# A weight row's tail and a unit's output in one transfer each, and W of a later unit begun at the head of a pass

## The chip, the cores and the metric

The kernel runs on one NeuronCore of a Trainium2 chip. That core has a matrix engine (TensorE, PE in the profile; PEld is its weight load), a vector engine (VectorE, DVE), a scalar engine (ScalarE, ACT), a general engine (GpSimd, POOL) and a sequencer that issues transfers (SyncE, SP). Transfers move between HBM and the on-chip memory SBUF through 16 DMA engines. Products of PE land in PSUM, a small memory in banks, from which DVE or ACT must read them before a bank can be used again.

The metric is the time of one execution on the device in microseconds (us), the median of several runs. Less is better.

## What is computed

Two parts follow each other. The first is a linear recurrence over 768 time steps for 4 batches and 8 heads of width 40; the second is a mixture of four experts, applied to the result as 3072 rows of 320.

```python
# attention: r, k, v, w, a, b are [batch 4, heads 8, seq 768, 40]
for t in range(S):
    y[:, :, t] = einsum('bhd,bhde->bhe', r_t, state)
    Sa = einsum('bhde,bhe->bhd', state, a_t)
    state = state * w_t[..., None] - einsum('bhd,bhe->bhde', Sa, b_t)
    state = state + einsum('bhd,bhe->bhde', v_t, k_t)
x = y.transpose(0, 2, 1, 3).reshape(3072, 320)

# mixture: w1 [4, 320, 1024], w2 [4, 1024, 320], p = domain_probs normalised by row
for e in range(4):
    h = maximum(x @ w1[e], 0)
    out += p[:, e:e+1] * (h @ w2[e])
```

All data are float32.

## The kernel before

**Units and passes.** The sequence is cut into 12 chunks of 64 tokens (L = 64). A unit is one chunk of two batches, so 128 rows on the 128 partitions; there are 24 units, two per chunk. The main loop (L1074 on) makes one pass per unit. Pass u works on several units at a time: it finishes the recurrence's step for one unit, prepares the next (`merge`, `begin_step`), advances the work inside the chunk of unit u + 2 (`within`, L402, with the substitution on POOL), and begins the loads of unit u + 3. Between these, at the places called `gap`, it issues pieces of the mixture for units that are already done, so that PE has products at all times.

**Loads of a unit.** Each input of a unit is loaded in one or two layouts. `load` (L198) brings W, B, K, V by tokens into `natW`, `natB`, `natK`, `natV` with two transfers each (L202). `load_raw` (L206) brings W, A, V, R by heads into `rawW`, `rawA`, `rawV`, `rawR`, four transfers each for W and A and eight each for V and R (L223); there is one buffer of each. DVE turns these round with a transpose (L241) into `G` (from rawW), `AT`, `VT` and `RT`. In the kernel before, pass u begins rawW, rawA, natW, natB, natK, natV of unit u + 3 in its middle, after `gap(1)`, and puts the transfers of rawV and rawR in a list called `later`, from which `mix` takes a few after each piece of the mixture.

**Step.** `step` (L628) makes `Y` of a unit (L707 adds, L712 scales with G). From the third chunk on, Y goes to the mixture's input `xT` with twelve transfers on SP from SBUF to SBUF (L736). On DVE, the same stage holds the work inside a later chunk: the reciprocal `gp` (L432), `n_tok` (L468), `k_tok` (L472), whose transposes PE makes (`pNT`, `pKT`, L79).

**Weights.** The first layer's weights don't stay on the chip. They stream as pieces: `load_piece` (L281) brings half an expert, 512 columns of w1 of 320 rows, into `w1p`, of which there are two buffers (the first pieces also use tiles called `sums`). Rows 0 to 255 come in one transfer of 512 KB, `main`, in runs of 2048 bytes. The last 64 rows, the tail, are held as two halves of the columns on partitions 0 to 63 and 64 to 127, and come in two transfers of 64 KB each, in runs of 1024 bytes (L300). 104 pieces are loaded: eight for each chunk, and sixteen for the first, whose two units are taken one after the other. In `up_last` the products on the tail come first for a piece: `ph` with lhsT = `last`, 64 x 64. The second layer's weights stay on the chip.

**Outputs.** `down_1` and `down_2` make the second layer's products, and DVE adds them into a tile `osb` of 128 rows for each unit (L786). `store` (L788) writes it to `out` in two transfers of 64 rows, 80 KB each, as the two batches lie apart in HBM. For the last chunk, `down_2_at_end` stores the last unit in two halves of the columns, the second with ACT as a second issuing engine.

**Order.** In the first passes (u < 5), and for what is put in `keep_in_program_order` (the pieces, the `later` transfers), each engine's order is as written. Elsewhere a scheduler places the instructions by its own estimate; so a change of a transfer's place in the code is not always a change of place on its engine. SP issues nearly all transfers, 1327 of 1336, one after the other; a transfer that waits, on a store's `osb` for instance, holds up those behind it. An even steady pass has natW, natV, twelve of xT, then pieces with natB, natK, rawW, rawV, rawA and rawR between; an odd pass has rawR, the four stores of a chunk, the last rawR, natW, natV, twelve of xT.

## Time and profile before

| | |
|---|---|
| median of three runs | 1124.0 us (1122.39 to 1124.98) |
| the profiled execution | 1122.36 us |
| its span, first to last instruction | 1120.2 us |
| granted TensorE clock, mean | 0.986 |
| transfers of w1p: mains and tails | 95 of 512 KB, 190 of 64 KB |
| transfers of pieces into `sums` tiles, mains | 9 of 512 KB |
| bytes read from HBM, written | 111.79 MB, 3.93 MB |

The profile is of one execution. Busy times are sums over the span; the DMA share is the mean over the core's 16 DMA engines. In a timeline a line gives the start, the duration, the engine, the line of the code, the operation, what it writes and reads, and how many instructions of the kind stand together; brackets at the end give the idle time before, and what ended it. For SP (SPq) the duration is that of issuing, not of moving the data.

## The change

There are three edits.

- The tail of a piece comes in one transfer. Its target is the 128 partitions of the tile's last 256 columns; its source is the 64 rows of w1 seen as two halves of columns, [2, 64, 256].
- `store` writes a unit's output in one transfer, from the 128 partitions of `osb` to an [2, 64, columns] view of `out`. Its parameter is now the issuing engine; at the end of the kernel the right half of the last unit is issued by ACT as a whole.
- rawW and natW of unit u + 3 are begun at the head of pass u, ahead of `run(w_next)` and so of the step whose end places xT. The rest, rawA, natB, natK and natV, is begun where all of them were. `begin(u + 3)` moves with it.

```diff
--- before.py
+++ after.py
@@ -290,13 +290,10 @@
         q.main = t[:, 0:2 * HF * P].rearrange("p (g c) -> p g c", g=2)
         q.last = t[:, 2 * HF * P:PIECE].rearrange("p (f c) -> p f c", c=P)
         cols = slice(x * HF * P, (x + 1) * HF * P)
-        moves = [(q.main, moe_w1[e, 0:2 * P, cols].rearrange("(g p) c -> p g c", p=P))]
-        for i in range(2):
-            half_cols = slice((2 * x + i) * HF // 2 * P, (2 * x + i + 1) * HF // 2 * P)
-            moves.append(
-                (q.last[i * DT:(i + 1) * DT], moe_w1[e, 2 * P:DM, half_cols].rearrange("d (f c) -> d f c", c=P))
-            )
-        for to, src in moves:
+        for to, src in (
+            (q.main, moe_w1[e, 0:2 * P, cols].rearrange("(g p) c -> p g c", p=P)),
+            (t[:, 2 * HF * P:PIECE], moe_w1[e, 2 * P:DM, cols].rearrange("d (i c) -> i d c", i=2)),
+        ):
             tc.keep_in_program_order(nc.sync.dma_start(out=to, in_=src))
         pieces.append(q)
 
@@ -785,10 +782,9 @@
         else:
             nc.vector.scalar_tensor_tensor(out=to, in0=p, scalar=sc, in1=to, op0=ALU.mult, op1=ALU.add)
 
-    def store(q, osb, cols=slice(0, DM), second=nc.sync):
-        for i, eng in enumerate((nc.sync, second)):
-            row = q.b[i] * S + q.c * L
-            eng.dma_start(out=out[row:row + L, cols], in_=osb[i * L:(i + 1) * L, cols])
+    def store(q, osb, cols=slice(0, DM), eng=nc.sync):
+        rows = out.rearrange("(b s) d -> b s d", b=B)[q.b[0]:q.b[1] + 1, q.c * L:(q.c + 1) * L, cols]
+        eng.dma_start(out=rows, in_=osb[:, cols])
 
     def outputs():
         return sb.tile([P, DM], FP32, name="osb", tag="osb", bufs=2)
@@ -1089,6 +1085,9 @@
         early = u < EARLY
         if early:
             begin_later(len(later))
+        if u + 3 < NU:
+            go(load_raw(begin(u + 3), "W"))
+            load(units[u + 3], "W")
         run(w_next, 99 if early else 1)
         run(s, 1)
         gap(0)
@@ -1116,8 +1115,8 @@
             gap(1)
 
         if u + 3 < NU:
-            go(load_raw(begin(u + 3), "WA"))
-            load(units[u + 3], "WBKV")
+            go(load_raw(units[u + 3], "A"))
+            load(units[u + 3], "BKV")
             later.extend(load_raw(units[u + 3], "VR"))
         run(w, 2)
```

`down_2_at_end` is the caller that passes the issuing engine; its text is unchanged: `store(qs[1], osb[1], right, nc.scalar)`.

## What the change was predicted to do

> **What bounds the kernel now.** I read the page's engine shares first, then busy time by stage, then the timelines of SP, VectorE (DVE) and TensorE (PE) over one pass, because the change touches only SP's transfers and the question is which wait on one of them reaches PE.

> ```profile
> span 1120.2 us, 38531 instructions
> PE 1076.8 (96%) x16100; PEld 961.0 (86%) x16100; DVE 757.0 (68%) x1553; ACT 353.2 (32%) x956; POOL 501.9 (45%) x1272
> q1 hardware_dynamic: 265416, 119.12, 44.0%
> ```
> ```profile
> 43.00:86.00 43.00, 38.61 (x632) 31.82 (x631) 24.73 (x64) 14.56 (x45) 2.50 (x6) 1.00 0.88 253
> 258.00:301.00 43.00, 39.99 (x532) 36.24 (x531) 28.88 (x57) 11.84 (x31) 19.81 (x51) 0.96 0.48 114
> 516.00:559.00 43.00, 43.00 (x670) 39.02 (x669) 31.37 (x64) 14.35 (x39) 21.80 (x56) 1.00 0.46 112
> 559.00:602.00 43.00, 42.85 (x671) 38.80 (x670) 31.22 (x64) 14.47 (x39) 22.00 (x56) 1.00 0.47 108
> ```

> The second fence is busy time by stage: stretch, length, then PE, weight loads, DVE, ACT, POOL, clock, DMA share, GB/s. PE is full in the steady passes (43.00 and 42.85 of 43), so there is nothing to gain there and each us of PE waiting is a us of run time. Gaps lie only early: 38.61 while DMA is 0.88 busy, and 39.99 at 258–301. From the second I looked for what DVE and PE wait for:

> ```profile
> 264.11 0.93 DVE L241 STREAM_TRANSPOSE G<-rawW 128x256 f32<-128x256 f32 x2 [5.37 <-DMA rawW<-in_w_dram]
> 311.97 0.93 DVE L241 STREAM_TRANSPOSE G<-rawW 128x256 f32<-128x256 f32 x2 [7.98 <-DMA w1p<-in_moe_w_dram]
> 269.49 0.87 PE L76 MATMUL ph<-xT,w1p 64*64 64x256 f32 x11 [3.01 <-issue]
> 318.16 1.47 PE L76 MATMUL ph<-xT,w1p 64*64 64x256 f32 x11 [4.05 <-issue]
> ```

> (start, duration, what, and in brackets the idle before and its releaser). W arrives late twice, DVE stands, the output sums behind it free PSUM late, and PE loses 3.01 + 4.05 us. This is what the W edit can take away. Then one odd pass in the steady part, which holds both stores:

> ```profile
> 550.37 1.56 SPq L300 DMA_DIRECT2D w1p<-in_moe_w_dram  x3
> 551.98 1.53 SPq L223 DMA_DIRECT2D rawR<-in_r_dram  x3
> 554.16 3.29 SPq L791 DMA_DIRECT2D out_dram<-osb  x4
> 557.49 0.58 SPq L223 DMA_DIRECT2D rawR<-in_r_dram  x1
> 561.53 8.95 SPq L736 DMA_DIRECT2D xT<-Y  x12
> 570.59 1.66 SPq L300 DMA_DIRECT2D w1p<-in_moe_w_dram  x3
> ```
> ```profile
> 556.74 2.15 DVE L432 RECIPROCAL gp<-gp 128x320 f32<-128x320 f32 x1
> 558.80 0.69 DVE L707 TENSOR_TENSOR Y<-pdy,RS 128x256 f32<-128x256 f32 x2
> 561.64 0.61 DVE L472 TENSOR_TENSOR k_tok<-natK,gp 128x320 f32<-128x320 f32 x1
> 562.18 0.70 DVE L241 STREAM_TRANSPOSE RT<-rawR 128x512 f32<-128x512 f32 x1
> 565.38 0.60 PE L79 MATMUL pKT<-ident,k_tok 128*128 128x128 f32 x4
> 578.13 1.08 PE L76 MATMUL ph<-xT,w1p 64*64 64x256 f32 x15
> ```

> The reader is to see that the last rawR is issued behind the four stores, that RT reads it only at 562.18, that PE takes k_tok 3.1 us after it is ready (562.25 to 565.38), and that piece 52 is wanted at 578.13, its tails having landed at 575.15.

> [...] In q1, 265416 packets less 245360 data packets, counted from the shapes, leave 20056 completion packets. [...] The source of the new tail is [2, 64, 256] and the target of the new store [2, 64, 320][...].

> **The change part by part.** Packet times are from the trace's packet records of SP's queue: 2048 B 106 ns mean, 1024 B 46 median and 54 mean, stores' 1280 B 89 mean, 95 median and 55 the lowest twentieth, loads' 1280 B 58, 640 B 29 to 43.

> Removed: 129 transfers (104 tails, 25 stores). SP's issue falls by about 0.5 us each; one pass loses about 3 of some 45 us, and SP isn't the bound. I count nothing.

> Tails: 64 KB twice over 16 engines was 8 rows an engine, 0.4 us. [...]64 x 46–54 ns = 2.9–3.5 us. A tail so lands about 2 to 3 us later. Slack from a tail's landing to the first product on it is 11–39 us for pieces 0 to 15; later 8–13 and 4.5–8 us, but for the piece right behind xT (every fourth) only 1.8–4.6, median 2.8, and 0.6 for piece 96. In the even passes this is just hidden: +1.5 in all (bounds 0 and +3).

> Stores, odd pass[...]. Main of piece 51 till 553.3; its tail till 556.5; three rawR till 557.0; store 1, 64 x 60 ns = 3.84, till 560.8; store 2 till 564.7; then the last rawR, landed at about 565.7 in place of 560.9. For the 60 ns I take a value near the load's 58, [...]not the 89 mean under 16 engines; 55 and 95 are the bounds. In the changed program's order DVE's RT stands directly behind the reciprocal in seven odd passes with the last rawR behind the stores, ahead of Y, n_tok and k_tok, where the kernel before has it behind k_tok. So DVE waits from 558.9 to 565.7, 6.8 us. Queued behind it: Y (which xT awaits), n_tok, k_tok. k_tok ends at 566.4 (RT) + 3.3 = 569.7 in place of 562.25, 7.5 later; less 3.1 of slack PE waits 4.4 at pKT. xT starts at 567.8 in place of 561.53, takes its 9 us, piece 52 is issued at 576.9, its main lands 4.1 later (the latency from the trace) at 581.0, and its tail, 64 x 50 ns behind the main on two engines, at 583.7. The first product on it is due at 578.13 + 4.4 = 582.5: 1.2 more. Together 5.6 us a pass, times 7 = 39.2. Bounds: 4.2 (55 ns) and 8.9 (95 ns) a pass, 29 and 62. The pass before these (RT still behind Y): +1 (0 to 2).

> Start: nine pieces by 74 us put 9 x 2.6–3 = 23–27 us [...]; loads of unit 3 come some 8 us later, against 8 to 16 us of slack: +1.5 (0 to 3).

> W first: six transfers a pass go ahead of run(w_next). In steady passes SP's order stays as it was, so nothing; around the two waits of DVE above W goes ahead of xT's twelve, so these gaps close: -6 of the 7.06 us that PE shows there (bounds -9, with smaller bits before, and -3, if the next wait on the same PSUM comes up). It moves the pieces and xT back by 6 x 0.5 us = 3 us of issue in early passes, where the pieces have 11 us and more.

> End: before, the last stores go out at 1114.96 to 1117.48 and the last lands at 1119.36. Now osb0's 64 rows, then left and right half on the same two engines: 3.84 + 2 x 64 x 31 ns = 7.8, from about 1116.2, plus 0.8 to land = 1124.8: +5.4, uncovered (5 to 9).

> Sum: 39.2 + 1 + 1.5 + 1.5 + 5.4 - 6 = +42.6. The profiled execution took 1122.36 (span 1120.2 and 2.16 around it), so 1165.0; the median of the runs is 1124.0, 1.6 above, so 1166.6. I take 1166.

> **The rivals.**
> B, worse: a transfer on SP waits until an earlier one in its rotation of eight completion semaphores has landed, so late tails also stop SP. Then the even passes and the pieces' 1.8 us slacks are hit too: about 2.5 us in 16 more places, +40, 1206. For: xT's piece has little slack. Against: the tails of the other three pieces have 4.5 us and more.
> C, hidden: two engines suffice, since store packets at the 55-ns floor or a rawR that isn't the one RT needs let RT be in time. The end's +5.4 and small bits remain against W's -6, with 0 to 1 us in the odd passes: 1124 to 1132, take 1129. For: DMA is only 0.46 busy. Against: 10.5 us of work is in front of rawR on two engines and DVE's slack is gone.
> D, faster: the new transfers are split by rows over all 16 engines after all. Tail and store then cost what they did, and W first closes the two PE gaps: 1124.0 - 7 = 1117. It decides if tails land within 4.5 us of their issue. For: 3.01 and 4.05 us are real. [...]
> That the change doesn't do what it says: in the steady passes the W part indeed moves nothing; this is within the forecast.

> **How the numbers follow.** Forecast 63%, B 13, C 13, D 8, others 3. The forecast's own range is 1122.4 + 1.6 + (29 + 0 + 0 + 0 + 5 - 9 = 25) = 1149 to 1124 + (62 + 2 + 3 + 3 + 9 - 3 = 76) = 1200. To leave out no more than 2 in 10 it goes to 1128 below (most of C) and 1205 above (part of B). A measurement tells 0.2% (2.2 us) from no change: faster is D with a piece of the rest, 0.09; the same, C at its low end, 0.05; slower 0.86.

> **What would show it.** Right: SP's queue shows tails landing 5 to 7 us after issue, stores 5 to 10 us; DVE waits 5 to 8 us at RT for rawR in seven odd passes; PE waits 4 to 5 us at pKT and about 1 us on the piece behind xT; the waits of 5.37 and 7.98 us for W are gone; the last landing is some 8 us after the last store. Wrong: PE 43.00 of 43 in the steady stretches, or tail packets seen on 16 engines. RT's waits without PE's would mean that PE had more work in hand than pKT's 3.1 us shows.

## The result, and the profile after

| | before | changed |
|---|---|---|
| median of four runs | 1124.49 us (1122.39 to 1125.57) | 1234.14 us (1232.46 to 1236.42) |
| profiled execution, its span | 1122.36, 1120.2 us | 1232.75, 1230.6 us |
| granted TensorE clock | 0.986 | 0.954 |

The changed kernel takes 1.0977 times as long (95% interval 1.0941 to 1.1013): 110 us more, where 42 us more were predicted. The direction is right and the size is not.

The page of the changed kernel: span, busy time of the engines, the one SP queue, and the chain that ended last.

```profile
span 1230.6 us, 38343 instructions
...
PE 1112.6 (90%) x16100; PEld 990.7 (81%) x16100; DVE 751.9 (61%) x1553; ACT 353.4 (29%) x956; POOL 489.6 (40%) x1272
...
q1 hardware_dynamic: 261496, 119.06, 39.5%
...
PE 53%; DMA 17%; DVE 10%; SPq 8%; ACT 4%; issue 4%; POOL 2%; DVEq 0%; ACTq 0%; POOLq 0%
```

PE's time splits into two parts. It was idle 1120.2 - 1076.8 = 43.4 us and is now idle 1230.6 - 1112.6 = 118.0 us, which is 74.6 more; and it is busy 35.8 us longer with the same 16100 products. Both parts together are the 110.4 us that the span grew. Transfers make up 17% of the chain, where they were 2%, while their 16 engines are less busy on average than before (39.5% against 44.0%). So something waits for single transfers; over all 16 engines throughput isn't short. For two engines alone this mean says nothing.

The packets show two engines under the new tails and stores, which the prediction had assumed when it put 64 rows of a tail on each. Packets of 4 bytes in this queue number 20056 before and 16200 now; the data packets fall only from 245360 to 245296, as half of the last store is on ACT. At the end of the kernel those of one transfer stand apart: the last store on ACT leaves 16 of them before and 2 now. If each of the 208 tails and 49 stores on SP left 16, and each of the 104 tails and 24 stores on SP now leaves 2, that is 257 x 16 - 128 x 2 = 3856 fewer, just the difference. The tails' own packets (13312 of the queue's 13360 packets of 1024 bytes) say the same. In 59% of the time in which any of these is under way, more than three are before, and up to 20; now it is more than three in 0.7% of it, and just two in 73%. The last two stores, one of SP and one of ACT, have 256 packets of 640 bytes and together just two under way in 3.0 of 3.7 us, so both queues' stores share two engines there. Which two of the 16 these are isn't shown.

Busy time by stage of the changed kernel, for the stretches shown of before (stretch, length, PE, weight loads, DVE, ACT, POOL, clock, DMA share, GB/s):

```profile
43.00:86.00 43.00, 39.40 (x641) 32.74 (x641) 24.71 (x63) 15.27 (x47) 2.49 (x6) 1.00 0.74 227
...
258.00:301.00 43.00, 41.15 (x644) 36.56 (x643) 30.62 (x60) 13.84 (x39) 19.09 (x49) 0.96 0.48 114
...
516.00:559.00 43.00, 38.08 (x624) 34.05 (x623) 26.67 (x57) 11.83 (x32) 21.49 (x55) 0.92 0.41 96
559.00:602.00 43.00, 40.48 (x531) 36.88 (x532) 23.22 (x44) 13.01 (x36) 18.86 (x51) 0.96 0.46 110
```

The steady stretches, which were full (43.00 and 42.85) at clock 1.00, have lost 2.4 to 4.9 us each, and their clock is 0.92 to 0.96. Early, where DMA was 0.88 busy, PE has lost nothing.

One odd pass of the changed kernel, SP's issues (start, duration of issuing, what):

```profile
576.94 0.99 SPq L297 DMA_DIRECT2D w1p<-in_moe_w_dram  x2
577.97 0.94 SPq L223 DMA_DIRECT2D rawV<-in_v_dram  x2
578.96 2.86 SPq L223 DMA_DIRECT2D rawR<-in_r_dram  x4
583.32 1.32 SPq L297 DMA_DIRECT2D w1p<-in_moe_w_dram  x2
584.68 1.42 SPq L223 DMA_DIRECT2D rawR<-in_r_dram  x3
591.24 2.82 SPq L787 DMA_DIRECT2D out_dram<-osb  x2
594.11 0.53 SPq L223 DMA_DIRECT2D rawR<-in_r_dram  x1
...
603.02 9.00 SPq L733 DMA_DIRECT2D xT<-Y  x12
612.12 1.10 SPq L297 DMA_DIRECT2D w1p<-in_moe_w_dram  x2
```

and what DVE, ACT and PE wait for in it (in brackets the idle time before, and its releaser):

```profile
584.63 0.71 DVE L241 STREAM_TRANSPOSE VT<-rawV 128x512 f32<-128x512 f32 x1 [5.11 <-DMA rawV<-in_v_dram]
585.27 0.73 DVE L397 COPY_PREDICATED SX<-mask_up,pxr 128x256 f32<-128x256 int32 x2
...
600.82 0.71 DVE L241 STREAM_TRANSPOSE RT<-rawR 128x512 f32<-128x512 f32 x1 [4.76 <-DMA rawR<-in_r_dram]
```
```profile
585.71 1.50 ACT L689 COPY RS<-pxr 64x256 f32<-64x256 f32 x4 [11.12 <-DVE SX L397]
587.23 1.09 ACT L767 ACTIVATE hs<-ph 128x512 f32<-128x512 f32 x2
```
```profile
587.88 2.33 PE L76 MATMUL p<-w,a 128*128 128x160 f32 x8 [2.41 <-ACT hs L767]
...
604.01 0.63 PE L79 MATMUL pNT<-ident,n_tok 128*128 128x128 f32 x4 [1.60 <-DVE n_tok L465]
...
619.62 1.21 PE L76 MATMUL ph<-xT,w1p 64*64 64x256 f32 x16 [2.32 <-DMA w1p<-in_moe_w_dram]
```

There are three stalls in a pass. The second and third are the prediction's: RT stands for the last rawR behind two stores, so n_tok is late and PE idles 1.60 us; and the piece behind xT is late by 2.32 us. The first isn't in the prediction at all. The last two rawV are issued right behind the tail of the pass's third piece. VT reads them; it stands in DVE's order ahead of SX; ACT's RS waits for SX; ACT's hs, which has nothing to do with V, is queued behind RS; and PE waits for hs. A late rawV so stops the mixture.

What made rawV late can be read from the semaphore events. The third piece's tail, issued at 577.38, landed at 584.10; the last two rawV, issued right behind it with no wait of SP between, landed at 584.31 and 584.51. In each of the last 16 passes the last rawV landed 0.4 to 0.6 us behind this tail. From issue to landing it took 3.0 us at the median of these passes before, and 6.0 now. SP also issues it later, set against the moment when DVE is free for VT: 1.4 us ahead of that at the median, where it was 2.7. Whether SP's own waits are in this smaller part isn't shown.

Before, the same chain was there in some passes, with nothing to spare:

```profile
547.41 0.71 DVE L241 STREAM_TRANSPOSE VT<-rawV 128x512 f32<-128x512 f32 x1 [0.87 <-DMA rawV<-in_v_dram]
```
```profile
548.49 1.50 ACT L692 COPY RS<-pxr 64x256 f32<-64x256 f32 x4 [6.89 <-DVE SX L400]
550.01 1.08 ACT L770 ACTIVATE hs<-ph 128x512 f32<-128x512 f32 x2
```

VT already waited 0.87 us for rawV in the kernel before, and hs ended at 551.1 when PE began the products that need it at 551.26. In this pass a later rawV would have come through to PE. The changed kernel differs in one more way: DVE has VT ahead of SX in all of the last 16 passes, where the kernel before has it there in 7 of them and behind SX in the others. Not all of VT's waiting reaches PE: in the changed kernel VT waits 85 us in all, and PE 38 us for hs.

## The experiments

The theory after the profile, K: tails and stores sit on two engines; what is queued behind them on those engines is late; and the readers of these late loads (VT, RT, PE's products on a piece) make the loss. W first is a gain. Rivals: O, that the order of the instructions, which the scheduler changes with the transfers, or SP's rotation of eight completion semaphores (the traces of before and of the changed kernel show landings on eight) makes it; B, that two engines are short of throughput, wherever a transfer stands; N, that it is the number and size of the transfers. (B is here, and in the expectations, another theory than the prediction's B.)

**One part at a time.** Each of the three edits alone in the kernel before. First, W first:

```diff
+        if u + 3 < NU:
+            go(load_raw(begin(u + 3), "W"))
+            load(units[u + 3], "W")
         run(w_next, 99 if early else 1)
```

> Only W of unit u+3 is begun at the head of the pass; tails and stores are in two transfers each, as before. Theory K (what costs is that tails and stores sit on two engines, and what is queued behind them is late; W is innocent): 1118 to 1127 us, PE idle in all as before within 5 us. Rival W (the earlier W pushes pieces and reorders DVE, and that is a good part of the +110): 1140 or more.

Measured: 1113.34 us (ratio 0.9906, 0.9879 to 0.9934). W alone gains 11 us, more than K had expected (1118 to 1127 us), and this is the fastest of the kernels. Its stages where PE had gaps:

```profile
258.00:301.00 43.00, 43.00 (x671) 39.22 (x670) 33.88 (x68) 15.90 (x45) 22.04 (x55) 1.00 0.49 117
301.00:344.00 43.00, 43.00 (x673) 39.14 (x672) 31.04 (x63) 13.41 (x36) 21.66 (x55) 1.00 0.44 105
```

Before, these had 39.99 and 38.95 us at clock 0.96. rawW is now issued at 236.16 instead of 260.77, ahead of xT, and DVE's G at 252.78 does not wait.

Then the tails alone in one transfer (the diff's first edit):

> Only the tails are in one transfer each. Theory K, as it now stands after the profile of the changed kernel: rawV stands behind a tail in every pass, VT on DVE waits for it (54.6 us of waits for rawV in the changed kernel, 7.5 before), and this is half or more of the loss: 1160 to 1190 us, VT waits 40 us or more, RT waits under 10 us. Rival S (the prediction's picture: tails are just hidden and the stores make the loss): 1124 to 1130.

Measured: 1202.07 us (1.0711, 1.0661 to 1.0761), more than either expected. The waits of this kernel (engine, line, what was waited for: us in total, times, longest):

```profile
DVE VT L241 <- DMA rawV<-in_v_dram: 43.0, 11, 8.8
...
PE p L76 <- ACT hs L767: 41.6, 13, 6.1
...
DVE VT L241 <- DMA rawR<-in_r_dram: 22.1, 4, 6.6
...
DVE VT L241 <- DMA w1p<-in_moe_w_dram: 21.1, 3, 8.0
...
PE ph L76 <- DMA w1p<-in_moe_w_dram: 8.4, 5, 3.0
```

VT waits 86 us in all and PE 41.6 us for hs, which it did for 0.8 us before. The tails, which the prediction had as hidden, are the largest part. PE is idle 56.2 us longer than before, 40.8 of it for hs, and it is busy 22.9 us longer.

The stores alone in one transfer (the second edit):

> Only the stores are in one transfer each. Theory K: RT waits for the last rawR behind two stores of 3.3 us each, 4 to 5 us in seven or more odd passes, and the end is 5.6 us later: 1145 to 1165 us, VT waits under 15 us. Rival T (tails are all of it): only the end, 1128 to 1132. Rival S (stores are all of it): 1200 or more.

Measured: 1166.77 us (1.0376, 1.0343 to 1.0409), a little above what K expected. Its waits:

```profile
DVE RT L241 <- DMA rawR<-in_r_dram: 30.6, 7, 4.9
...
DVE VT L241 <- DMA rawV<-in_v_dram: 23.8, 8, 5.5
...
PE pNT L79 <- DVE n_tok L468: 21.2, 8, 3.4
...
PE p L76 <- ACT hs L770: 11.4, 12, 2.7
```

Seven waits at RT, as predicted. VT waits 41.7 us for rawV and rawR, where under 15 was expected: DVE has it ahead of SX in 14 of the last 16 passes here. The parts add up: -11.3 + 77.4 + 42.1 = +108 (against a median of 1124.65 for the kernel before), and the whole is +110. So there is no large effect of the edits on each other.

**The stores in another queue.** The changed kernel, with the stores issued from ACT, whose transfers stand in a queue of their own (q10 on the page, 3330 packets in the changed kernel; SP's is q1):

```diff
-    def store(q, osb, cols=slice(0, DM), eng=nc.sync):
+    def store(q, osb, cols=slice(0, DM), eng=nc.scalar):
```

> The changed kernel, with its single stores issued from ACT, so that they stand in another ring of the same two engines and no load of SP is queued behind them. Theory K: RT's wait falls from 35 us in all to under 12, the tails' part and the end's stay: 1195 to 1215 us. Rival B (the two engines are short of throughput, so whose ring it is doesn't matter): 1228 to 1240. A cost of ACT's waiting for osb would show as ACT idle before hs; it would add up to 10.

Measured: 1213.66 us (1.0791, 1.0756 to 1.0827), some 20 us less than the changed kernel. RT's waits for rawR are gone (35.0 us in the changed kernel), though the stores are as narrow as in the changed kernel; so that stall came from the place in SP's queue, and B falls for the stores. VT's waits stay (95 us in all, 85 in the changed kernel).

**Loads four at a time.** To take rawV and rawR out of the shadow of the third tail and of the stores, I began the queued loads by four instead of three after each piece:

```diff
-            begin_later(3 if n > 1 else 6)
+            begin_later(4 if n > 1 else 6)
```

in e2, in e3, in the changed kernel and, as the control, in e1:

> Single tails only, and the queued loads of rawV and rawR are begun four instead of three at a time after each piece, so that all eight rawV stand behind the second piece's tail and all eight rawR behind the third's: the transfer that VT waits for leaves the third tail's shadow. DVE still has VT ahead of SX. Theory K (rawV behind the third tail stalls VT, and with it SX, RS, hs and PE): VT's waits fall below 15 us, PE's idle ahead of p<-w,a below 10 (from 41.6), 1135 to 1165 us; what is left is PE waiting for pieces (23.0 us with e2) and its clock. Rival O (the order VT before SX that comes with single tails, or the slow rotation of semaphores on SP, is the cause, not what stands behind which tail): 1190 to 1205.

> Single stores only, with the loads begun four at a time, so that no rawR stands behind a store. Theory K: RT's waits vanish, the end's 5.6 us and some 0 to 5 us for natW, natV and xT behind the stores stay: 1126 to 1138 us. Rival B (the stores take throughput from everything for 6.7 us a chunk, whoever stands behind them): 1155 to 1168 as with e3.

> The changed kernel with the loads begun four at a time. Theory K: what e5 and e6 leave, less the 11 us of W: 1130 to 1165 us. Rivals O and B: above 1200.

> Two transfers each for tails and stores, W first, loads four at a time: the control, and a candidate for the fastest. Theory K: the order of the loads matters only behind narrow transfers, PE is full in the steady passes of e1 already: 1109 to 1118 us, no different from e1's 1113.3. If four at a time is itself worth something: below 1108.

Measured: 1392.28, 1354.06, 1403.60 and, for the control, 1335.54 us. The control alone is 222 us slower than e1, so none of the four says anything on K, and the expectation of the control was wrong. One pass of its profile suggests why:

```profile
605.18 0.71 DVE L241 STREAM_TRANSPOSE VT<-rawV 128x512 f32<-128x512 f32 x1 [4.25 <-DMA rawV<-in_v_dram]
605.82 1.93 DVE L547 STREAM_TRANSPOSE M<-blocks 128x1024 f32<-128x1024 f32 x1
...
628.56 0.61 DVE L596 STREAM_TRANSPOSE Qc<-Z 128x256 f32<-128x256 f32 x1 [14.39 <-POOL Z L585]
...
629.57 1.45 DVE L880 TENSOR_TENSOR a<-hs 128x512 f32<-128x512 f32 x2
```
```profile
632.67 7.51 PE L76 MATMUL ph<-xT,w1p 64*64 64x256 f32 x30 [11.51 <-issue]
```

In the control the scheduler has put VT ahead of M, from which POOL starts its substitution, and Qc ahead of the mixture's adds. VT then waits 4.25 us, POOL starts late, DVE stands 14.39 us at Qc with the adds behind it, and PE idles 11.51 us. That VT's place alone makes the 222 us wasn't tested; if the reading is right, the place of one DVE instruction is worth more here than the whole change.

**A shift that leaves DVE's order alone.** So the loads stay as they are, and the narrow transfers move: a tail goes behind the next three queued loads, and the stores go one piece of the mixture later.

```diff
-            tc.keep_in_program_order(nc.sync.dma_start(out=to, in_=src))
+            if to is q.main or not hold[0]:
+                tc.keep_in_program_order(nc.sync.dma_start(out=to, in_=src))
+            else:
+                held.append((to, src))
...
+            hold[0] = len(later) > 0
             piece()
+            hold[0] = False
             for begin_store in ready:
                 begin_store()
             begin_later(3 if n > 1 else 6)
+            begin_tails()
...
-                    store(q, o)
+                    stores.append(lambda q=q, o=o: store(q, o))
```

`begin_tails` issues what is in `held`. In the steady passes DVE's order of VT, SX, RT and Y is that of e2, of e3 and of the changed kernel.

> Single tails only, as in e2, and where loads of rawV and rawR are queued, the tail of a piece is begun behind the next three of them: the last two rawV are then ahead of the third piece's tail in place of behind it. DVE's order in the steady passes is that of e2 (VT ahead of SX). Theory K (what stands behind a tail on two engines is late): VT's waits for a load under 25 us in all (86 with e2), PE's idle ahead of p<-w,a under 10 us (41.6), 1135 to 1170 us; PE's waits for pieces (23.0 us) and the clock after them stay. Rival O (DVE's order or SP's rotation of semaphores): 1185 to 1205.

> Single stores only, as in e3, begun one piece of the mixture later, so that the last rawR is ahead of them; DVE's order is that of e3 (RT ahead of Y, VT ahead of SX). Theory K: RT's waits fall from 30.6 to under 5 us, PE's idle ahead of pNT from 21.2 to under 6, the end's 5.6 us stay and VT's waits too: 1130 to 1148 us. Rival B (the stores hold everything up for 6.7 us a chunk wherever they stand): 1160 to 1170.

> The control: e1 with both deferrals, tails and stores in two transfers each. DVE's order in the steady passes is the changed kernel's in all passes (RT ahead of Y, VT ahead of SX). Theory K: the order alone costs little when nothing lands late: 1110 to 1122 us. Rival O: 1140 or more.

> The changed kernel with both deferrals. Every transfer is as narrow as in the changed kernel, only what stands behind it differs. Theory K: RT's and VT's waits mostly gone, 1130 to 1165 us. Rivals O and B: above 1200.

| | without | with the shift | ratio to before, with it |
|---|---|---|---|
| tails alone (e2, e9) | 1202.07 | 1153.62 | 1.0252 (1.0203 to 1.0301) |
| stores alone (e3, e10) | 1166.77 | 1143.88 | 1.0177 (1.0137 to 1.0216) |
| W first alone (e1, e11) | 1113.34 | 1119.40 | 0.9952 (0.9935 to 0.9969) |
| all three (changed, e12) | 1234.14 | 1159.08 | 1.0320 (1.0260 to 1.0379) |

All four lie where K expected them. The same narrow transfers, in the same number, cost 75 us less when the tails go behind the next loads and the stores behind the last rawR. The control has the changed kernel's order of these on DVE and is only 6 us slower than e1, so this order alone isn't the cause. Nor does the other half of O, SP's waiting for an earlier transfer's semaphore, explain the most of it: the 3.0 us by which the last rawV lands later come after its issue. In the waits of e9, PE's wait for hs has fallen from 41.6 to 6.2 us and the wait for pieces has grown:

```profile
DVE VT L241 <- DMA rawR<-in_r_dram: 31.4, 12, 4.3
...
PE ph L76 <- DMA w1p<-in_moe_w_dram: 14.9, 9, 2.9
...
DVE VT L241 <- DMA rawV<-in_v_dram: 8.5, 5, 4.2
...
PE p L76 <- ACT hs L777: 6.2, 11, 1.6
```

One number was missed: VT still waits 40 us in all, where under 25 was expected. But these waits are shorter (2.4 us on average against 4.8), and little of them comes through to PE. In e10 RT's waits are gone, as expected.

**The width alone.** Single transfers also change the number of transfers. Each 64-row transfer of the kernel before can instead be cut into 60 + 4 rows or into 62 + 2; between these two the number, the bytes and every engine's order are the same. That the first pair stays wide and the second becomes narrow was assumed before the runs; for the tails the packet counts below bear it out:

```diff
-            moves.append(
-                (q.last[i * DT:(i + 1) * DT], moe_w1[e, 2 * P:DM, half_cols].rearrange("d (f c) -> d f c", c=P))
-            )
+            for lo, hi in ((0, 62), (62, DT)):
+                moves.append((
+                    q.last[i * DT + lo:i * DT + hi],
+                    moe_w1[e, 2 * P + lo:2 * P + hi, half_cols].rearrange("d (f c) -> d f c", c=P),
+                ))
```

and likewise in `store`.

> The kernel before with each tail half cut into 60 and 4 rows (four transfers a piece where there were two). [...] Theory K: the width is nearly what it was, so 1120 to 1145 us, the upper part for 208 more transfers on SP and the order that DVE gets. Every engine's order is the same as in the next kernel. Rival N (the loss came with the number, size or order of transfers, not with the engines that they use): no difference between this and the next, within 10 us.

> The same with 62 and 2 rows[...]; number, order and bytes of the transfers are those of the kernel before this one. Theory K: 64 rows of a piece stand on each of two engines as with the single tail, so slower than the 60-row kernel by 40 to 90 us. Rival N: within 10 us of it.

> The kernel before with each store of 64 rows cut into 60 and 4 rows[...]. Theory K: 1122 to 1138 us. Rival N: as the next one, within 8 us.

> The same with 62 and 2 rows[...]. Theory K: as with the single stores, slower than the 60-row kernel by 20 to 45 us (e3 lost 42, of it 5.6 at the end). Rival N: within 8 us of it.

| | 60 + 4 rows | 62 + 2 rows | difference |
|---|---|---|---|
| tails | 1139.40 (1138.40 to 1144.64) | 1191.60 (1178.19 to 1194.94) | +52 |
| stores | 1131.54 (1130.03 to 1132.71) | 1140.42 (1136.92 to 1143.77) | +9 |

The pages of the two tail kernels count 266040 and 262920 packets in SP's queue, where before has 265416: 3 more and 12 fewer for each of the 208 tails of before, whose rows, and so the data packets, stay as many. With the 16 packets of 4 bytes that such a tail left there, this makes 19 for 60 + 4 rows and 4 for 62 + 2. For the stores no such count is shown.

For the tails, width alone is worth 52 us, within K's 40 to 90, and N falls. It takes another way to PE here, as VT has another place in both kernels of the pair: SP's waits for landed weights before it can issue other loads grow from

```profile
SPq L223 <- DMA w1p<-in_moe_w_dram: 39.9, 56, 2.0
...
SPq L302 <- DMA w1p<-in_moe_w_dram: 4.6, 6, 2.6
```

to

```profile
SPq L223 <- DMA w1p<-in_moe_w_dram: 139.1, 135, 2.1
...
SPq L302 <- DMA w1p<-in_moe_w_dram: 41.1, 53, 2.0
```

and PE's waits for a piece from 0.3 to 14.5 us. For the stores, 9 us is below the 20 to 45 expected, and 5.2 of it is at the end of the kernel (183.1 us from the last reciprocal of DVE to the end of the span against 177.9). In this pair RT stands behind k_tok in the odd passes, as in the kernel before, and waits only 9.6 us for rawR. So the part of the 42 us that RT makes takes both: a late rawR, and RT ahead of Y, where the scheduler put it when the stores became one transfer. Either alone is cheap (some 4 us here without the end, 6 us in e11).

## Why the prediction was wrong, point by point

**The step that failed** is the tails: "In the even passes this is just hidden: +1.5 in all", with +1.5 more at the start. Measured alone, the tails cost 77 us. The delay itself was priced well: a tail was put 2 to 3 us late, and from the semaphore events it landed 6.7 us after issue at the median, against 3.8 before. What failed is the list of who waits. The prediction held a tail's delay against the slack of the tail's own reader, the products on the piece. It did not hold it against the readers of the loads queued behind the tail, though it did just that for the rawR behind the stores. rawV stands behind the third tail of each steady pass, and the profile of before showed VT waiting for it already (0.87 us in the pass that was read, six times in all). Nor did it ask where VT would stand, as it did for RT: the changed order has VT ahead of SX in every steady pass, which lets the delay through to hs and PE. e9 shows what the loads behind the tail are worth: with the last two rawV ahead of it, 48 of the 77 us are gone, in the same order of VT and SX, though the tails are begun no earlier. e9 also halves SP's waits for landed weights (L223 and the pieces' line: 72 us in e2, 38 in e9), so not all of the 48 need be VT's. The some 30 us that remain go along with PE's waits for pieces, 14.9 us in e9; how they divide further wasn't tested.

**Stores, odd pass: the number is right by luck.** 39.2 + 1 and 5.4 at the end were predicted, 46 in all; alone they cost 42. The stall at RT is there, but 4.4 us a time and not 6.8 (two stores of 64 rows landed 3.33 us apart, 52 ns a row instead of the 60 taken). It reaches PE at pNT, not at pKT, with 2.7 us a time and not 4.4: 17.7 us of new idle time (21.2 against 3.5), where 7 x 4.4 = 30.8 were put. The 1.2 us a pass for the piece behind xT need the narrow tail too; e3 doesn't show them, and the changed kernel has 10.2 us of such waits in 6. What fills the gap in e3 was not foreseen: 10.6 us more of waiting for hs, behind VT, and 9.9 us of PE being busy longer. (The working has a slip too: 581.0 + 64 x 50 ns is 584.2, not 583.7.)

**End: right.** From the last reciprocal of DVE to the end of the span, 183.1 us against 177.5: +5.6 where +5.4 was predicted.

**W first: right in mechanism, too small.** -6 was predicted, from the 7.06 us of gaps that PE shows; -11.3 was measured (e1). The waits of 5.37 and 7.98 us at G are gone as foreseen, and PE's idle time fell by 5.9 us in the profiled execution. The sum forgot that its busy time falls too, from 1076.8 to 1073.6 us: before, the clock was halved for 3.41 us right behind each of the two gaps (from 270.51 and from 318.30), and in e1 it isn't.

**Start: small, but above its bounds.** +1.5 (0 to 3) was predicted. From the first to the sixth reciprocal of DVE, a mark that each pass has, it is 169.13 us against 163.95: +5.2. How much of this the tails make isn't shown: it is +3.6 with the tails alone (e2), but +3.3 in e15 too, whose tails are as before. The stretch that was feared, 43 to 86 us, has lost nothing (39.40 us of PE against 38.61).

**"Each us of PE waiting is a us of run time": too little.** PE's idle time explains 74.6 of the 110 us; the other 35.8 is PE being busy longer with the same products. The trace's record of the clock accounts for nearly all of that: PE was busy for 89.7 us in stretches at half clock, against 23.7 before, and half of the difference, 33.0 us, is time lost. The same reckoning gives 23.7 us for e2 and 10.8 for e3, where PE is busy 22.9 and 9.9 longer. So each us of waiting brought nearly half a us more in the changed kernel (35.8 / 74.6 = 0.48), which no term of the sum had; in e3 it was 0.29, in e10 0.13.

**The rivals.** B, a late tail that also stops SP, was given 13% and 1206 us. Its mechanism is in the waits: SP waits for landed weights 35.0 us at L223 and 35.5 at L297, against 10.9 and 1.8 before. But in the changed kernel PE's wait for hs behind VT (38.4 us) is larger than its wait for pieces (10.2), and most of rawV's delay comes after its issue. C (hidden) is refuted by the times of e2 and e3, D (16 engines after all) by the packets.

## What to carry to other kernels

A transfer that becomes slower should be held against the slack of every reader of what is queued behind it on the same engines, not only of its own reader; an instruction that already waits a little for such a load is where the loss came out here. Before two transfers are merged, see how widely the merged one is spread: here 128 rows in one transfer, as [2, 64], left 2 packets of 4 bytes where each half had left 16, and went two packets at a time; and no run shows a gain from the 129 issues saved. Of the three edits, only the one that changed no shape was good, and alone (e1) it beats both kernels.

## What the runs showed of the hardware

```profile
584.68:588.09 3.41, 1.00 (x7) 0.76 (x6) 1.32 (x3) 2.33 (x6) 2.86 (x8) 1.00 0.61 189
588.09:591.51 3.42, 3.42 (x14) 3.42 (x14) 3.16 (x6) 0.23 (x1) 3.03 (x6) 0.50 0.10 26
591.51:594.92 3.41, 3.41 (x116) 3.24 (x118) 3.15 (x6) 1.24 (x5) 2.93 (x7) 1.00 0.10 23
499.34:502.76 3.42, 1.43 (x11) 1.18 (x9) 1.82 (x5) 0.00 (x0) 0.36 (x2) 1.00 0.24 48
502.76:506.17 3.41, 2.04 (x70) 1.75 (x72) 3.38 (x11) 1.16 (x2) 0.28 (x1) 1.00 0.04 12
506.17:509.58 3.41, 3.41 (x88) 2.84 (x80) 3.27 (x9) 0.25 (x1) 2.11 (x4) 1.00 0.11 29
```

PE's wait of 2.41 us for hs, until 587.88, falls into one step and leaves PE 1.00 us of work in it. The whole next step is granted 0.50, which costs 3.41 x 0.5 = 1.7 us more; then the clock is full again. A longer wait, 3.37 us until 504.13, is shared by two steps (1.43 and 2.04 us of work), and the clock stays full. Counted over the steps at full clock in the traces of all 18 kernels, from 40 us on: after each of the 158 in which PE was busy for less than 0.40 of the step the clock was halved; after 38 of the 249 between 0.40 and 0.75; after none of the 5308 above that. (PE's busy time is as the profile models it.)

**Two rows more, 52 us.** In e13 and e14 each half of a tail is cut in two, with 19 packets of 4 bytes for 60 + 4 rows and 4 for 62 + 2. The second kernel is 52 us slower (1191.60 against 1139.40 us). What in a transfer's shape sets its spread isn't shown.

What stays open: why cutting the tails into 60 + 4 rows costs 15 to 17 us against the kernel before. PE's busy time grew by 21 us there at nearly the same clock (0.988 against 0.986), and DVE's order was another; no run separates the two. The trace says where the time is, not why: the 1408 `ph` products on the tail (64*64 64x256) are each as long as before (386 ns against 385), but together take 120.9 us of PE in place of 103.2, so 4.5 of them ran side by side on average and not 5.3.
